# Two units' running sums as products with a triangle, and a written-out order for the first six steps

## The chip, the cores and the metric

The kernel runs on one core of a Trainium2 chip. Its engines are called by the names of the profile: PE (TensorE, the matmuls), DVE (VectorE), ACT (ScalarE), POOL (GpSimd) and SP (SyncE, which here only issues DMAs). Each engine works through its own instructions in the order of the program and waits on semaphores for the others. The metric is the device time of one execution in microseconds (us).

## The reference

A gated linear recurrence is followed by a layer of eight experts, of which each token uses one. B = 4, H = 8 heads, S = 768 tokens, D = 48.

```python
f = 1.0 / (1.0 + np.exp(-f_logit))
for t in range(S):
    state = f[:, :, t, :, None] * state + einsum('bhd,bhe->bhde', k[:, :, t], v[:, :, t])
    y[:, :, t] = einsum('bhd,bhde->bhe', q[:, :, t], state)
x = y.transpose(0, 2, 1, 3).reshape(B * S, H * D)          # (3072, 384)
expert_idx = argmax(x @ w_gate); gate_w = softmax probability of that expert
out = gate_w * (relu(x @ w1[expert_idx]) @ w2[expert_idx])  # F = 1024
```

## The kernel before

The recurrence is computed in blocks of 128 tokens. A **unit** is one block of tokens of two batches with all heads: there are twelve (NU = 12), and unit u continues the state of unit u - 2. In SBUF a unit of q, k and f lies with the channels on the partitions (a pair of heads, each padded from 48 to 64) and eight segments of 128 tokens along the free dimension; v lies with tokens on the partitions. Within a unit the steps are, with the name that the change's list gives each and the function that does it:

- `lf lk lq lv`: the loads (`load`), all on SP's queue. f has two buffers, k three, q four, v three; a load waits until the last reader of its buffer is done.
- `exp`, `ln` (`steps`, `log`; ACT): ln(1 + exp(-f)), which is the negative logarithm of the gate, into a tile g.
- `scan` (`total`; DVE): the running sum of g over the tokens of each segment. One scan of a unit goes over 128 x 1032 elements: each segment has a column of zeros in front, and a minimum with a tile `cap` starts the sum anew there and bounds it.
- `r` and `dec` (`growth`, `decay`; ACT): exp of the sum and exp of its negative.
- `byr` (k times r, POOL, in unit 0 DVE), `byd` (q times decay, DVE). A POOL product waits by hand for a DVE instruction that is known to be a good place (`routed`).
- `ends`, `last` (POOL): the last columns of the sums and of the decay.
- `sc` (`score`; PE): k times q, four PSUM banks; `mask` (DVE): the lower triangle of it is copied by a predicate.
- `kp`, `keep` (`keys` on PE, copied by ACT): k with tokens on the partitions; `dp` (`added`; PE): its product with v, the addition to the state; `upd`, `updp` (`update`; DVE adds, POOL multiplies by the last decay).
- `wi` (`within`; PE, two halves a and b) and `bef` (`before`; PE): the two parts of the output, within the unit and from the state, into one PSUM tile yt; `set` (`settle`; ACT) copies it.
- `xp`, `lay` (`rows` on PE, with a small reduction on DVE for the gate; `lay` on ACT): the output by tokens and the gate's logits.
- `oh`, `wgh`, `place`, `send` (`Route`): the choice of expert for a pair of units, the place of each token's row, and the indirect DMA that sends it there.

Some PSUM tiles (`turns`: kp, dp, xp) take turns on two banks, so each waits for the reader of the last but one.

The units overlap by software: a loop over n = 1 to NU + 1 does, in each turn, the scores of unit n, the sums of unit n + 2, the exp and ln of unit n + 3, the output of unit n - 1 and the rows of unit n - 2, each engine in program order (`manual_schedule`). The steps of units 0 to 3 that lie ahead of the loop are written out before it, and the turns n = 1 and n = 2 differ from the others by conditions. Before the first products PE runs 24 products of a zero tile (`warm`), and 12 more later; their result is not used. The experts' matmuls follow after the loop.

The constants come in three transfers. A mask and the unit matrix are loaded first, through ACT's queue (`load_first_consts`). All others come later, by SP (`load_consts`, L174), and `load_gate` (L180) then writes the gate's weights into the same tile with four small transfers; the first of these waits for the transfer of the constants:

```python
for a, r in halves:
    for b, cols in enumerate((slice(XW, WX), slice(0, E))):
        nc.sync.dma_start(wx[r, :, cols], ...)      # wx is a view of the constants' tile
```

SP's order before: f0, k0, q0, f1, k1, q1, f2, v0, f3, k2, v1, q2, q3, constants, k3, f4, v2, f5, gate, q4, k4, v3, f6, three transfers of `pad` to DRAM, k5, and so on.

Of the kernel before, what the change touches and what calls it, by code (L numbers as in the profile page):

```python
# [10 lines left out]
F32 = mybir.dt.float32  # L11
I32 = mybir.dt.int32
U8 = mybir.dt.uint8
AF = mybir.ActivationFunctionType
OP = mybir.AluOpType
# [12 lines left out]
CR = C + 1  # L28
DM = H * D
# [44 lines left out]
RMAX, RTOP = np.log(1e18), np.log(1e19)  # L74

# [43 lines left out]
def _bc(ap, axis, n):  # L119
    shape = list(ap.shape)  # L120
    shape.insert(axis, n)
    return ap[tuple([slice(None)] * axis + [None])].to_broadcast(shape)
# [3 lines left out]
def kernel(  # L126
# [8 lines left out]
    fu: bass.AP,  # L135
    vu: bass.AP,
# [283 lines left out]

    with ExitStack() as st:
# [9 lines left out]

        cap = wk.tile([128, SEG, CR], F32, name="cap", bufs=1)
        nc.vector.memset(gsum, 0.0)
        nc.vector.memset(cap, RTOP)
        nc.vector.memset(cap[:, :, 0:1], 0.0)
# [8 lines left out]
        for g in decays:  # L444
            nc.vector.memset(g[:, :, 0:1], 0.0)
        units = [{} for _ in range(NU)]
        routed = []
        SYNC = mybir.DependencyInfo(mybir.DependencyClass.Sync, mybir.DependencyReason.DATA)
# [8 lines left out]
        def load(u, names, parts=(slice(None),)):  # L457
            x = units[u]
            for n in names:
                src = {"q": qu, "k": ku, "f": fu, "v": vu}[n]  # L460
                if n == "v":
                    x[n] = ld.tile([128, 2, H, D], F32, name=n, bufs=3)
                else:
                    x[n] = held[n][u % len(held[n])]
                for part in parts:
                    nc.sync.dma_start(x[n][:, part], src[u][:, part])

        whole, ab = slice(0, SEG), (slice(0, HP), slice(HP, SEG))

        def steps(u, part=whole, logs=True):  # L470

            x = units[u]
            x["g"] = decays[u % len(decays)]
            g = x["g"][:, part, 1:CR]
            most = gsum[:, u, 1 if part == ab[1] else 0]
            nc.scalar.activation(
                g, x["f"][:, part], AF.Exp, scale=-1.0, accum_out=most.unsqueeze(1)
            )
            if logs:
                log(u, part)  # L480

        def log(u, part=whole):
            g = units[u]["g"][:, part, 1:CR]
            nc.scalar.activation(g, g, AF.Ln, bias=1.0)  # L484

        def total(u, part=whole):

            x = units[u]
            if "sum" not in x:
                x["sum"] = wk.tile([128, SEG, CR], F32, name="sum")  # L490
            nc.vector.tensor_tensor_scan(  # L491
                x["sum"][:, part].rearrange("p s c -> p (s c)"),
                x["g"][:, part].rearrange("p s c -> p (s c)"),
                cap[:, part].rearrange("p s c -> p (s c)"),
                0.0,
                OP.add,
                OP.min,
            )

        def growth(u, part=whole):  # L500

            x = units[u]
            if "r" not in x:
                x["r"] = wk.tile([128, SEG, C], F32, name="r", bufs=1)
            nc.scalar.activation(x["r"][:, part], x["sum"][:, part, 1:CR], AF.Exp)  # L505

        def by_r(u, part=whole, on=nc.gpsimd):
            k = units[u]["k"][:, part]
            ins = on.tensor_tensor(k, k, units[u]["r"][:, part], op=OP.mult).ins  # L509
            if routed:  # L510

                tc.add_manual_dep(ins, routed.pop().name, SYNC, reason="the port of both")

        def ends(u):
            nc.gpsimd.tensor_copy(rend[:, u], units[u]["sum"][:, :, C])

        def decay(u, part=whole):
            x = units[u]
            x["dec"] = x["g"][:, :, 1:CR]
            nc.scalar.activation(  # L520
                x["dec"][:, part], x["sum"][:, part, 1:CR], AF.Exp, scale=-1.0
            )

        def last_decay(u):
            x = units[u]
            x["last"] = wk.tile([128, SEG], F32, name="last", bufs=3)
            nc.gpsimd.tensor_copy(x["last"], x["dec"][:, :, C - 1])  # L527

        def by_decay(u, part=whole):
            x = units[u]  # L530
            q = x["q"][:, part]
            nc.vector.tensor_tensor(q, q, x["dec"][:, part], op=OP.mult)  # L532
# [32 lines left out]
        def within(u, a):  # L565

            x = units[u]
            if a == 0:
                x["yt"] = yt
            for p, h, _ in heads():  # L570
                nc.tensor.matmul(  # L571
                    x["yt"][DP * (h ^ a) : DP * (h ^ a) + D, a, p],
                    lhsT=x["v"][:, a, 2 * p + h],
                    rhs=x["at"][:, a, h, p],
                    start=p == 0,
                    stop=x["old"] is None,
                    skip_group_check=True,
                )
# [38 lines left out]
        def update(u):  # L617

            x = units[u]
            new = wk.tile([128, SEG, D], F32, name="state", bufs=4)  # L620
            last = _bc(x["last"], 2, D)
            if x["old"] is None:
                nc.vector.tensor_copy(new, x["dp"])
            else:
                nc.vector.tensor_tensor(new, x["dp"], x["old"], op=OP.add)
            states[u % 2] = new
            return lambda: nc.gpsimd.tensor_tensor(new, new, last, op=OP.mult)
# [70 lines left out]
        load(0, "f", ab)  # L698
        load(0, "kq")
        load(1, "f")  # L700
        load_first_consts()
        load(1, "kq")
# [6 lines left out]

        warm(24)  # L710
        for part in ab:
            steps(0, part)
            total(0, part)
        load(2, "f")
        load(0, "v")
        for part in ab:
            growth(0, part)
            by_r(0, part, nc.vector)
            decay(0, part)
            by_decay(0, part)  # L720
        ends(0)
        last_decay(0)
        for part in ab:
            steps(1, part)
        load(3, "f")
        load(2, "k")
        load(1, "v")
        load(2, "q")
        load(3, "q")
# [44 lines left out]
        score(0, 0)  # L774
        score(0, 1)
        keys(0)
        warm(12)
        for part in ab:
            total(1, part)
        for a in range(2):  # L780
            for h in range(2):
                mask(0, a, h)
        for part in ab:
            growth(1, part)
            by_r(1, part)
        for part in ab:
            decay(1, part)
            by_decay(1, part)
        ends(1)
        last_decay(1)  # L790
        steps(2)
        total(2)
        keep(0)
        steps(3, logs=False)
        growth(2)
        load_consts()
        load(3, "k")
        load(4, "f")
        load(2, "v")
        load(5, "f")  # L800
        load_gate()

        for n in range(1, NU + 2):
# [3 lines left out]
            rt = None  # L807
            if here < NU:
                units[here]["old"] = states[here % 2]
            if 2 <= last:  # L810
                settle(last)
            if later and later[0] < NU - 1:
                later[1].weigh()
# [3 lines left out]
            if ahead and n != 2:  # L817
                by_r(n + 1)
                ends(n + 1)
# [7 lines left out]
            if n == 1:  # L827
                units[0]["old"] = None
                added(0)
                update(0)()  # L830
            if ahead and not 1 < n < 4:
                decay(n + 1)
                last_decay(n + 1)
# [3 lines left out]
            if n == 2:  # L837
                growth(n + 1)
                by_r(n + 1)
                ends(n + 1)  # L840
            if 1 < n < 4:
                decay(n + 1)
                last_decay(n + 1)
# [4 lines left out]
            if n == 1:  # L848
                log(3)
                within(0, 0)  # L850
                within(0, 1)
                settle(0)
# [6 lines left out]
            if 2 < n < NU - 2:  # L859
                total(n + 2)  # L860
            if n == NU - 2:
                by_decay(n + 1)
            first_half = 1 < n < NU - 2
            if first_half:
                within(back, 0)
            if 0 <= last:
                rt = rows(last, later[1] if later else None)
                lay(last)
# [6 lines left out]
            if n == 2:  # L875
                total(n + 2)
# [13 lines left out]
            if n == 2:  # L890
                settle(1)
            if n + 2 < NU and n != 1:
                growth(n + 2)
# [7 lines left out]
            if n == 1:  # L901
                total(3)
# [15 lines left out]
            if n == 1:  # L918
                load(n + 3, "q")
# [4 lines left out]
            if 1 < n and n + 3 < NU:  # L924
                load(n + 3, "q")
            if n + 5 < NU:
                load(n + 5, "f")
            if n == 1:
                load_first_pads()
# [398 lines left out]
```

## Time and profile before

| | us |
|---|---|
| median of 10 runs | 390.13 (389.79 to 391.0) |
| the profiled execution | 389.82 |
| its span, first to last instruction | 388.0 |
| PE busy in the span | 375.7 (97%) |
| DVE, ACT, POOL busy | 169.6, 102.9, 115.8 |
| scans (L491), 14 | 28.9 in all; 2.29 a whole one, 1.23 a half |
| DMA until 25 us | about 400 GB/s |

A line of a timeline gives start and duration (us), engine, line of the program, operation, output and inputs, number of instructions, and in brackets how long the engine was idle before and what released it. A line of a chain gives start, duration and what ran. "L491" is line 491 of the kernel before. A matmul in float32 shows as two records.

### The profile page before, as it was taken

To read this page: it belongs to the slowest core of one execution; us is meant where nothing else is said; L and a number is where in the kernel's file an instruction comes from. 1 tells how busy PE (TensorE), PEld (TensorE's weight loads), DVE (VectorE), ACT (ScalarE), POOL (GpSimd) and SP (SyncE) were. 2 spreads that over 40 slices of the span, in tenths; PEclk is the share of its full clock that TensorE was granted. 3 is DMA by queue.
4 is the path that set the end of the run, shared out by engine and by line. 5 is a ranking of instruction groups with operands and counts; after the bars stand their busy time and mean duration, and the time that the engine had idled before them with its cause. 6 is when DMAs were issued, how large, how long until landed. Compare 5 with 4: busy or idle time off the path is not lost.

```text
span 388.0 us, 7727 instructions
## 1 busy us (share of the span) xinstructions
PE 375.7 (97%) x3062; PEld 264.1 (68%) x3062; DVE 169.6 (44%) x365; ACT 102.9 (27%) x190; POOL 115.8 (30%) x118
## 2 busy tenths in 40 slices
PE   7888999999999999999999999999999999999993
PEld 7877899999989778685555555654466466555452
DVE  6998988889764732112121131116412113111360
ACT  6888878785433001010100110000010000001000
POOL 5378868887706610101102101100210210210112
PEclk9999999999999999999999999999999999999998
DMA  7999667778973559795649899898163359994141
GB/s 282 395 364 362 202 228 250 249 240 305 386 247 125 208 135 308 193 318 108 195 148 387 227 394 395 215 399 241 41 231 126 102 181 390 396 416 155 24 182 43
DMA packets 51516, 95.05 MB, mean 245 GB/s; under 512 B 20824, under 2 KB 40731, under 8 KB 49424
## 3 DMA queue, kind: packets, MB, share of 16 engines
q1 hardware_dynamic: 48016, 84.76, 64.1%
q0 software_dynamic: 3168, 9.64, 6.7%
q8 instruction: 25, 0.41, 0.4%
q10 hardware_dynamic: 288, 0.08, 0.2%
q14 instruction: 19, 0.16, 0.1%
HBM read 79.46 MB, written 15.21 MB: 244 GB/s over the span
## 4 chain that ended last, share of the span: by engine, by line
PE 88%; DMA 5%; DVE 2%; ACT 1%; SPq 1%; issue 1%; POOL 0%; POOLq 0%; DVEq 0%; ACTq 0%
PE hps L316 28%; PE yps L332 24%; PE yps L1107 7%; PE xp L663 6%; PE yt L571 5%; PE s L543 4%; PE s L316 3%; PE hps L1081 3%; PE yp L332 3%; PE yt L592 3%; DMA fpack<-c_fpack 2%; PE dp L608 2%; PE kp L558 2%; DMA fpack<-in_moe_w_gate_dram 1%; DVE sum L491 1%; DMA f<-in_fu_dram 1%
## 5 line engine op out<-in xcount | busy, mean ns | idle before, releaser
L316 PE MATMUL hps<-xT,w1t 128*128 128x352 f32 (+2 forms) x384 | 110.1, 447 | 0.0
L316 PEld LDWEIGHTS hps<-xT,w1t 128*128 128x128 f32 x384 | 72.7, 190 | 37.2 <-issue 1.9
L332 PE MATMUL yps<-w2t,hT 128*128 128x384 f32 x288 | 94.4, 487 | 0.0
L189 POOL DMA_INDIRECT out_dram<-ysb,dst x24 | 23.3, 972 | 222.0 <-DVE ysb L343 213.9
L332 PEld LDWEIGHTS yps<-w2t,hT 128*128 128x128 f32 x288 | 54.6, 190 | 38.6 <-issue 1.5
L326 ACT ACTIVATE hT<-hps 128x352 f32<-128x352 f32 (+2 forms) x28 | 13.7, 490 | 200.7 <-PE hps L316 190.6
L328 DVE TENSOR_SCALAR hT<-hps 128x352 f32<-128x352 f32 (+2 forms) x28 | 15.6, 558 | 93.0 <-PE hps L316 93.0
L343 DVE TENSOR_SCALAR ysb<-yps,tg 128x384 f32<-128x384 f32 x22 | 13.6, 618 | 74.4 <-PE yps L332 55.7
L189 POOL DMA_INDIRECT xs<-xr,posi x24 | 32.2, 1342 | 18.9 <-DVE xT L299 12.9
L549 DVE COPY_PREDICATED at<-mpack,s 128x512 f32<-128x512 uint8 x48 | 31.0, 727 | 6.1 <-PE s L543 6.1
L509 POOL TENSOR_TENSOR k<-k,r 128x1024 f32<-128x1024 f32 (+1 forms) x12 | 26.5, 2215 | 19.3 <-ACT r L505 9.9
L491 DVE TENSOR_TENSOR_SCAN sum<-g,cap 128x1032 f32<-128x1032 f32 (+1 forms) x14 | 28.9, 2064 | 2.8 <-ACT g L484 2.8
L1107 PE MATMUL yps<-qw,hqT 128*32 128x192 f32 (+1 forms) x192 | 26.8, 380 | 0.0
L543 PE MATMUL s<-q,k 64*128 64x128 f32 x384 | 24.9, 279 | 1.7 <-POOL last L527 1.1
L663 PE MATMUL xp<-fpack,ys 128*128 128x104 f32 x192 | 25.1, 281 | 0.8 <-DMA fpack<-in_moe_w_gate_dram 0.6
L543 PEld LDWEIGHTS s<-q,k 64*128 64x128 f32 x384 | 22.5, 188 | 3.9 <-issue 1.5
L571 PE MATMUL yt<-at,v 128*48 128x128 f32 x384 | 25.1, 276 | 0.0
L663 PEld LDWEIGHTS xp<-fpack,ys 128*128 128x128 f32 x192 | 22.7, 192 | 2.7 <-issue 1.3
L571 PEld LDWEIGHTS yt<-at,v 128*48 128x48 f32 x384 | 20.0, 123 | 2.6 <-issue 1.5
L1107 PE MATMUL yps<-w2t,hT 128*32 128x384 f32 x192 | 21.4, 487 | 0.0
L1107 PEld LDWEIGHTS yps<-w2t,hT 128*32 128x32 f32 x192 | 7.6, 110 | 13.0 <-issue 12.5
L532 DVE TENSOR_TENSOR q<-q,g 128x1024 f32<-128x1024 f32 (+1 forms) x14 | 16.4, 1178 | 0.0
(114 smaller groups left out, 360.1 us busy)
## 6 DMA issues: line engine op xcount, KB each, us to landing
qw<-in_moe_w_dram SPq DMA_DIRECT2D x16, 1536.0 KB, 13.7
w1t<-in_moe_w_dram SPq DMA_DIRECT2D x8, 1536.0 KB, 7.2
w2t<-in_moe_w_dram SPq DMA_DIRECT2D x8, 1536.0 KB, 15.9
k<-in_ku_dram SPq DMA_DIRECT2D x12, 512.0 KB, 4.9
q<-in_qu_dram SPq DMA_DIRECT2D x12, 512.0 KB, 5.8
f<-in_fu_dram SPq DMA_DIRECT2D x11, 512.0 KB, 6.0
xs<-pad SPq DMA_DIRECT2D x8, 600.0 KB, 4.4
v<-in_vu_dram SPq DMA_DIRECT2D x12, 384.0 KB, 5.9
```

Of the source, the lines that this page charges most:

```text
L189: ins = nc.gpsimd.indirect_dma_start(out=dst, out_offset=bass.IndirectOffsetOnAxis(ap=idx, axis=0), in_=src, in_offset=None, bounds_check= ...
L316: nc.tensor.matmul(x["h"][:, f], lhsT=w[0][:, j, b * 128 : b * 128 + 128], rhs=x["xT"][:, j], start=j == 0, stop=j == KD - 1,)
L328: nc.vector.tensor_scalar(to, x["h"], 0.0, None, op0=OP.max)
L332: nc.tensor.matmul(yp, lhsT=x["hT"][:, f, t * C : t * C + C], rhs=w[1][:, f, :], start=f == 0, stop=f == NF - 1,)
L491: nc.vector.tensor_tensor_scan(x["sum"][:, part].rearrange("p s c -> p (s c)"), x["g"][:, part].rearrange("p s c -> p (s c)"), cap[:, part ...
L509: ins = on.tensor_tensor(k, k, units[u]["r"][:, part], op=OP.mult).ins
L532: nc.vector.tensor_tensor(q, q, x["dec"][:, part], op=OP.mult)
L543: nc.tensor.matmul(ps[h][:, p], lhsT=x["k"][r, s], rhs=x["q"][r, s], start=True, stop=True)
L549: nc.vector.copy_predicated(x["at"][:, a, h], _bc(causal, 1, HP), x["ps", a][h])
L571: nc.tensor.matmul(x["yt"][DP * (h ^ a) : DP * (h ^ a) + D, a, p], lhsT=x["v"][:, a, 2 * p + h], rhs=x["at"][:, a, h, p], start=p == 0, st ...
L663: nc.tensor.matmul(xp[:, p], lhsT=x["ys"][:, a, p], rhs=wx[:, p, 0:XW] if a else wx[:, p, E:WX], start=True, stop=True,)
L1107: nc.tensor.matmul(yp[r], lhsT=h[:, f, at : at + T], rhs=w[:, f, cols], start=f == 0, stop=f == NF - 1, skip_group_check=True,)
```

## The change

f of units 0 and 1 (`NATURAL = 2`) comes from an array `fn` that is laid out with tokens on the partitions, without padding (48 instead of 64 channels), in two halves. exp and ln write it into g with tokens on the partitions, and the running sum is then a product of g with an upper triangle of ones, which also turns it so that the channels lie on the partitions; the sums stay in PSUM, where r and decay read them. The bound of the sum moves into the product with k, as a minimum of r (both halves on DVE, in unit 1 too, where POOL did it before). The tile of ones is cast from the mask by DVE; the g tiles of units 0 and 1 are cleared as a whole.

```diff
-        for g in decays:
+        for g in decays[:NATURAL]:
+            nc.vector.memset(g, 0.0)
+        for g in decays[NATURAL:]:
             nc.vector.memset(g[:, :, 0:1], 0.0)
+        def more_consts():
+            nc.vector.tensor_copy(upto, causal)
+            nc.vector.memset(cap, RTOP)
+            nc.vector.memset(cap[:, :, 0:1], 0.0)
...
+                if n == "f" and u < NATURAL:
+                    flat = x[n].rearrange("p s c -> p (s c)")[:, 0 : SEG * 2 * D]
+                    x["fn"] = flat.rearrange("p (s h d) -> p s h d", s=SEG, h=2)
+                    for part in ab:
+                        nc.sync.dma_start(x["fn"][:, part], fn[u][:, part])
+                    continue
...
+        def summed(u, part):
+            x = units[u]
+            a = ab.index(part)
+            if u:
+                ps = turns("sum", [128, HP, C])
+            else:
+                ps = pss.tile([128, HP, C], F32, name="s")
+            x["sums", a] = ps
+            for p in range(HP):
+                nc.tensor.matmul(
+                    ps[:, p], lhsT=x["g"][:, HP * a + p, 1:CR], rhs=upto, start=True, stop=True
+                )
...
         def by_r(u, part=whole, on=nc.gpsimd):
             k = units[u]["k"][:, part]
+            if u < NATURAL:
+                port["latest"] = nc.vector.scalar_tensor_tensor(
+                    k, units[u]["r"][:, part], RMOST, k, op0=OP.min, op1=OP.mult
+                ).ins
+                return
...
         def ends(u):
-            nc.gpsimd.tensor_copy(rend[:, u], units[u]["sum"][:, :, C])
+            if u < NATURAL:
+                for a, part in enumerate(ab):
+                    nc.vector.tensor_copy(rend[:, u, part], x["sums", a][:, :, C - 1])
+            else:
+                nc.gpsimd.tensor_copy(rend[:, u], x["sum"][:, :, C])
```

The steps ahead of the loop and its turns n = 1 to 5 are gone; in their place stands a list of steps, by the names above with the number of the unit and a half or a part, and the loop begins at n = 6 without its special cases. `fill10` is ten products of the zero tile, `consts0`, `consts1` and `consts2` are the first constants, the other constants and `more_consts`, `gate` is `load_gate`, `pads` the transfers of `pad`. Each engine and queue takes its own steps in the order of the list:

```diff
+    FIRST_STEPS = """
+        consts0 lf0 lk0 lq0 lf1 lk1 lq1 consts2 fill10 exp0a ln0a scan0a exp0b lf2 lv0 ln0b scan0b
+        r0a byr0a dec0a byd0a r0b byr0b dec0b byd0b ends0 last0 exp1a ln1a exp1b lf3 lk2 lv1
+        lq2 lq3 consts1 gate0 ln1b sc0a scan1a scan1b sc0b r1a dec1a r1b dec1b mask0a byr1a
+        ends1 byd1a byr1b byd1b last1 sc1a fill2 kp0 mask0b exp2 ln2 keep0 scan2 exp3 r2
+        sc1b byr2 ends2 dp0 lk3 lf4 lv2 lf5 upd0 upd0p dec2 last2 kp1 lq4 lk4 keep1 mask1a
+        mask1b ln3 wi0a wi0b lv3 set0 exp4 lf6 pads0 byd2 dp1 upd1 scan3 sc2a upd1p kp2 sc2b
+        keep2 r3 ends3 byr3 dec3 last3 mask2a mask2b exp5 wi1a xp0 lay0 ln4 ln5 byd3 scan4
+        wi1b lk5 lv4 lq5 lf7 set1 r4 dp2 upd2 sc3a sc3b scan5 byr4 ends4 kp3 keep3 dec4
+        last4 mask3a mask3b exp6 ln6 wi2a wi2b lk6 lv5 xp1 lay1 byd4 oh1 r5 bef2 lq6 lf8 dp3
+        upd3 set2 wgh1 sc4a sc4b byr5 upd2p ends5 dec5 last5 kp4 keep4 mask4a mask4b scan6
+        exp7 ln7 wi3a xp2 lay2 byd5 place1 wi3b lk7 lv6 r6 dp4 upd4 bef3 lq7 lf9 set3 sc5a
+        sc5b byr6 upd3p ends6 upd4p dec6 last6 kp5 keep5 mask5a mask5b scan7 exp8 ln8 wi4a
+        wi4b lk8 lv7 xp3 lay3 byd6 oh3 r7 bef4 lq8 lf10 dp5 upd5 set4 wgh3 send5
+    """
...
+        for what, u, part in re.findall(r"([a-z]+)(\d+)([abp]?)", FIRST_STEPS):
+            DO[what](int(u), part)
...
-        for n in range(1, NU + 2):
+        for n in range(FIRST, NU + 2):
```

## The prediction

> **What bounds the kernel now.** I read the page first, then the chain of waits up to 60 us, then the timelines of PE, DVE, ACT and SP over the same stretch, and the DMA landings. On the page PE is busy for 97% of the span, and the chain that ended last is 88% PE. The room is in the first two of the forty slices. The chain says where it ends:
>
> ```profile
> 40.99 0.17 DVE lg L671
> 41.16 0.02 issue
> 41.19 0.49 ACT xr L693
> 41.67 0.04 issue
> 41.72 1.14 PE dp L608 x32
> 42.86 1.02 PE yt L592 x32
> 43.88 1.99 PE s L543 x32
> 45.86 1.02 PE kp L558 x8
> ```
>
> Up to 41.7 us the chain runs over DMA, ACT and DVE; from there every line to 108 us is PE, without a gap, one unit of the recurrence after the other. So a change in the first six steps is worth exactly what it does to the time at which PE takes up its closed row. I use one mark for this: the scores of unit 4 (43.81 us on PE's timeline). From there the order of PE's work is the same in both kernels but for a swap of neighbours, 18.37 us to the scores of unit 6, and then the same loop.
>
> What holds the row up before the mark is a group of full engines (in the slices 10:40 us DVE is busy 4.2 to 5.0 us of each 5, ACT 4.25 to 4.6) and the DMA queue, which moves about 400 GB/s until 25 us. The SP timeline, start, duration, queue and line, has the part that decides my forecast:
>
> ```profile
> 13.88 1.06 SPq L174 DMA_DIRECT2D fpack<-c_fpack  x1
> 15.06 0.37 SPq L466 DMA_DIRECT2D k<-in_ku_dram  x1
> 15.90 0.33 SPq L466 DMA_DIRECT2D f<-in_fu_dram  x1
> 16.75 0.33 SPq L466 DMA_DIRECT2D v<-in_vu_dram  x1
> 19.00 0.33 SPq L466 DMA_DIRECT2D f<-in_fu_dram  x1
> 22.76 1.79 SPq L180 DMA_DIRECT2D fpack<-in_moe_w_gate_dram  x4
> 24.65 0.39 SPq L466 DMA_DIRECT2D q<-in_qu_dram  x1
> ```
>
> SP's waits and the landings of two of these transfers (KB, us from issue to landing):
>
> ```profile
> SPq L180 <- DMA fpack<-c_fpack: 3.4, 1, 3.4
> fpack<-c_fpack SPq DMA_DIRECT2D x1, 473.5 KB, 8.9
> f<-in_fu_dram SPq DMA_DIRECT2D x1, 512.0 KB, 9.4
> ```
>
> The gate weights go into the tile that the constants fill, so SP stands still until the constants have landed (13.88 + 8.9 = 22.74), and what is behind in SP's program stands with it: q of unit 4 leaves at 24.65 although its buffer was free long before. But k3, f4, v2 and f5 are ahead of the gate and leave from 15.06 on. f4 lands at 15.90 + 9.4 = 25.3, and that already is a wait on ACT:
>
> ```profile
> 23.28 1.07 ACT L633 COPY ys<-yt 128x512 f32<-128x512 f32 x2
> 25.39 1.06 ACT L476 ACTIVATE g<-f 128x1024 f32<-128x1024 f32 x1 [1.04 <-DMA f<-in_fu_dram]
> 26.57 1.06 ACT L484 ACTIVATE g<-g 128x1024 f32<-128x1024 f32 x1
> ```
>
> **The change, part by part.**
>
> *Sums as products.* DVE loses four half scans of 1.23 us, 4.9 us. It gains k times r of unit 1 (two halves, 0.67 each by L509 on DVE, from POOL, where the two took 2.84), four copies of a last column and a cast of the triangle (0.1 to 0.2 each by the small copies, 0.7 in all). Net about 2.8 us off DVE. ACT: exp and ln of 384 instead of 512 elements take 0.48 instead of 0.63 (the 128x384 copy of L693), eight of them, 1.2 us. PE: 16 products, 32 records; 16 records of L663 take 1.96, so 1.0 per half and 4.0 in all, against 24 warm-up products fewer (48 records; the last 24 took 2.85). The memsets of two whole g tiles (0.92 each) lie before 4 us, ahead of the first exp at 3.6, and cost nothing; without that cover 1.8.
>
> *Where this would leave the first steps.* The ten warm-up products are not done at once: records 1 to 13 or so come at 0.2 us, the later ones at 0.113, so they end near 5.8 and the first sum at 6.9, where the first exp of sums now starts at 6.66. Unit 0 gains nothing. In unit 1 ACT's four exp and ln end at 11.15 instead of 11.75, and the 0.64 us wait for the scan goes: exp of unit 2 starts near 13.5 instead of 14.74, scan2 at 16.0 instead of 17.07, and mask, copies and ys of unit 0 each about 1.1 us earlier. ACT is through ys of unit 0 at 23.2 instead of 24.35. What is late next is f4.
>
> *The loads, re-ordered.* The written order puts the constants and the gate directly behind q3, and k3, f4, v2, f5, q4, k4 and v3 behind the gate. On SP they are all moved past a wait that they were ahead of. The constants land a little earlier: f of two units is 256 KB smaller (0.26 MB at some 405 GB/s, 0.65 us), so 22.1. It could be earlier by more, as nothing is queued behind them: at 22.74 the queue had moved 7.85 MB, 0.8 MB (2 us) more than was issued up to the constants, while the loads until 14 us landed with 0.37 MB (0.9 us) of such excess. That bounds the landing by 20.1 and 22.1; I take 21.6, nearest to the early loads. The gate's four issues hold SP for 1.89 (22.76 to 24.65), then k3 leaves at 23.5 and f4 at 23.95, into a queue that has run dry. Later in the trace f was issued right behind q in such a queue twice (43.94 and 44.36, 53.31 and 53.73) and landed 4.8 and 4.6 us after issue. The gate's own small packets go ahead of k3; in 25:28 us, with them, the queue moved 262 to 303 GB/s instead of some 405, which is 0.9 us lost, of which 0 to 0.5 would fall on k3. So f4 lands at L = 28.7, with bounds 27.0 and 29.7, against 25.3 now. It is queued ahead of everything on ACT: behind exp of unit 4 stand the copy of unit 2's keys, both exp of unit 3, exp of unit 5, rows of unit 0.
>
> *From f4 to the mark.* ACT in its new order, start to start by the rows of before: exp4 1.18, kn2 0.95, r3 0.95, decay3 0.95, exp5 1.18 (f5 lands 2.3 behind f4, in time), rows of unit 0 0.78, ln4 0.96: 6.95, and 0.05 to DVE: L + 7.0. DVE: scan4 2.22 and the state of unit 2 0.53: L + 9.75. PE has to wait for that state, as the second half of unit 3's keys takes the PSUM tile that it frees; then half the keys 0.5, two halves of unit 2's yt 2.0, xp of unit 1 1.96, the state's part of yt 1.02, dp of unit 3 1.05: 6.55, and the mark at L + 16.3. DVE beside it: scan5 2.29, four masks 2.5, gate sums 0.3 and q of unit 4 1.2 end at L + 16.0. Both branches end together, so neither can shorten it alone. At L = 28.7 the mark is at 45.0 instead of 43.81: +1.2 us. All that units 0 and 1 gained or lost before 23.2 goes into a wait of 5.5 us on ACT and is worth nothing; if f4 were there, ACT could start 2.2 us earlier than now. Contention adds 0 to 0.6 (one scan of before took 2.93 beside a POOL product, instead of 2.29).
>
> *A gap on PE.* PE has its first half of yt of unit 1 done near 26.9 and xp of unit 0 needs a PSUM tile that ACT's copy frees at L + 1.65 = 30.35: 3.4 us idle, where the longest idle of before was 1.1. What such a gap does to PE's rate no row of before shows; from the start of the trace (0.2 us per record in the first 3 us, then 0.113) the bounds are 0 and some 1.4 us over the 16 records. PE then has until L + 9.75 for xp, half of yt, dp, scores and half the keys, 6.5 us of work in 8.1; so I take 0, and up to 0.6 at the upper end. The Trainium skill, "TensorE: Matmul & The Clock Gate", Part 1 on the clock gate, says that an idle window of about 3.4 us halves PE's clock until as much sustained work has passed; by that rule the gap is on the edge, and since the slack holds the 1.4 us, the sum by the rule is still +1.2.
>
> **The sum.** The profiled execution took 389.82 us, its span is 388.0, with 1.8 around it; the median is 390.13. The rest of the span after the mark, 344.2, stays. 389.82 + 1.2 = 391.0 for a profiled execution, and 390.13 + 1.2 = 391.3 for the median.
>
> **The rivals.**
>
> A, faster: f4 is not late. For this the constants would have to land by some 20 us, or the loads to be held less by the gate. The mechanism is the one from which the rest follows: what counts is only L, and it decides at L = 27.5, where the mark is back at 43.8. If f4 came 0.65 before its present 25.3, the sum above gives 24.65 + 16.3 = 40.95, 2.9 us gained: 387.3. Against it: SP's wait of 3.4 us and q4's issue behind it stand in the trace; even the lowest bound, 27.0, gives 43.3 and only 0.5 gained. 15 in 100.
>
> B, no difference: f4 is late, but near its lower end (L of 27.2 to 27.9), as the constants land without company: 390.1. 12 in 100.
>
> C, slower still: PE's rate falls after the gap and the two scans run beside POOL's work, both of which are bounded above: L = 29.3 gives 45.6, plus 0.6 and 0.6, 46.8: +3.0, 393.1. 11 in 100.
>
> **How the numbers follow.** The forecast, L between 27.9 and 29.7 with the sum as it stands, gives +0.4 to +2.2 and has 62 in 100. A measurement of this kernel tells 0.2%, 0.8 us, from no change. Of the forecast 9 fall within that and 53 above; of A 13 below and 2 within; B is within, C above. Faster 0.13, same 0.23, slower 0.64. The range, 389.4 to 393.0, takes in the forecast, B, the weaker part of A and most of C, and leaves out some 17 in 100. The likeliest case's own range is 390.5 to 392.3.
>
> **What the changed profile would show.** On SP the four issues of the gate near 21.6, and k3 and f4 directly behind them at 23.5 to 24.0. On ACT one long wait for f, about 5 us, that ends near 28.7, and before it every step of units 0 to 2 earlier by 1 us. DMA running dry in 21:25 us. On PE a gap of some 3.4 us before the first L663-like product, and the scores of unit 4 at 45.0, without gaps after it. DVE with ten scans instead of fourteen. I am wrong if ACT's wait for f4 ends before 27.5, if the steps between it and unit 4's scores take other than 16.3 us, or if gaps come back after the mark.

## The result, and the profile after

The changed kernel takes 393.27 us (392.49 to 394.52, 9 runs) against 390.10 (30 runs): ratio 1.0084, 95% interval 1.0073 to 1.0095, 3.2 us slower. Its profiled execution took 392.67 with a span of 390.6, against 389.82 and 388.0.

In the lines below f4 is the f of unit 4 (the load `lf4`). `ys` is what `set` copies, `kn` what `keep` copies (kn2 is unit 2's), and `xr` are the rows that `lay` copies. The first steps' lines have other numbers in each kernel.

SP's timeline after the change (start, duration, queue, line, transfer):

```profile
13.57 0.43 SPq L178 DMA_DIRECT2D fpack<-c_fpack  x1
22.63 2.75 SPq L184 DMA_DIRECT2D fpack<-in_moe_w_gate_dram  x4
25.49 0.38 SPq L499 DMA_DIRECT2D k<-in_ku_dram  x1
25.96 0.38 SPq L499 DMA_DIRECT2D f<-in_fu_dram  x1
26.39 0.42 SPq L499 DMA_DIRECT2D v<-in_vu_dram  x1
26.86 0.42 SPq L499 DMA_DIRECT2D f<-in_fu_dram  x1
```

SP's longest wait (us in all, times, longest):

```profile
SPq L184 <- DMA fpack<-c_fpack: 8.5, 1, 8.5
```

And f4's way from issue to landing (KB, us):

```profile
f<-in_fu_dram SPq DMA_DIRECT2D x1, 512.0 KB, 4.2
```

SP issues nothing from 14.0 to 22.6 us. f4 leaves at 25.96 instead of 15.90 and lands at 30.1 instead of 25.3. The stretches 20:23 show the DMA running dry meanwhile. Each row gives the stretch, its length, the busy us of the five engines with counts, the clock granted to PE, and in the last two columns the share of the 16 DMA engines and GB/s:

```profile
20.00:21.00 1.00, 0.93 (x8) 0.67 (x7) 1.00 (x2) 1.00 (x2) 0.21 (x1) 1.00 0.73 284
21.00:22.00 1.00, 1.00 (x18) 0.86 (x18) 1.00 (x3) 1.00 (x2) 1.00 (x1) 1.00 0.22 87
22.00:23.00 1.00, 1.00 (x26) 1.00 (x22) 1.00 (x3) 1.00 (x3) 1.00 (x1) 1.00 0.02 8
```

ACT's timeline: the wait for f4 grew from 1.0 to 5.7 us, and the copies of unit 2's keys follow it.

```profile
23.46 1.07 ACT L700 COPY ys<-yt 128x512 f32<-128x512 f32 x2
30.20 1.06 ACT L515 ACTIVATE g<-f 128x1024 f32<-128x1024 f32 x1 [5.67 <-DMA f<-in_fu_dram]
...
31.25 1.05 ACT L630 COPY kn<-kp 128x512 f32<-128x512 f32 x2
```

PE's timeline, from the gap to the scores of unit 4:

```profile
27.61 1.08 PE L637 MATMUL yt<-at,v 128*48 128x128 f32 x16
31.87 3.13 PE L730 MATMUL xp<-fpack,ys 128*128 128x104 f32 x16 [3.19 <-ACT kn L630]
34.93 1.58 PE L637 MATMUL yt<-at,v 128*48 128x128 f32 x16
...
46.43 2.06 PE L610 MATMUL s<-q,k 64*128 64x128 f32 x32
```

In the kernel before, the same rows of unit 0 and the same scores stand at

```profile
28.93 2.00 PE L663 MATMUL xp<-fpack,ys 128*128 128x104 f32 x16 [0.62 <-DMA fpack<-in_moe_w_gate_dram]
...
43.81 2.06 PE L543 MATMUL s<-q,k 64*128 64x128 f32 x32
```

The mark, the scores of unit 4, is at 46.43 instead of 43.81: 2.62 us later. The span is 2.6 longer, so all of it arises before the mark; after it PE has no wait over 0.2 us in either kernel.

### The profile page after: what moved, and what is told of

Same layout as the page of the kernel before. It is cut to its first block, busy times and chain, and to the rows that moved or that the text cites. A ratio compares the mean times of both kernels' runs of the same rounds, so it can differ in the third digit from the quotient of the medians.

```text
span 390.6 us, 7692 instructions
## 1 busy us (share of the span) xinstructions
PE 375.9 (96%) x3046; PEld 264.1 (68%) x3046; DVE 168.1 (43%) x368; ACT 101.3 (26%) x190; POOL 108.2 (28%) x114
## 4 chain that ended last, share of the span: by engine, by line
PE 90%; DMA 4%; issue 1%; POOL 1%; ACT 1%; SPq 1%; POOLq 0%; DVE 0%; ACTq 0%
PE hps L320 28%; PE yps L336 24%; PE yps L1168 7%; PE xp L730 6%; PE yt L637 5%; PE s L610 5%; PE s L320 3%; PE hps L1142 3%; PE yp L336 3%; PE yt L658 3%; PE dp L674 2%; PE kp L625 2%; DMA f<-in_fn_dram 2%; DMA k<-in_ku_dram 2%; DMA f<-in_fu_dram 1%
## 5 line engine op out<-in xcount | busy, mean ns | idle before, releaser
L573 POOL TENSOR_TENSOR k<-k,r 128x1024 f32<-128x1024 f32 x10 | 23.8, 2375 | 24.6 <-ACT r L564 6.4
L730 PE MATMUL xp<-fpack,ys 128*128 128x104 f32 x192 | 26.3, 289 | 3.4 <-ACT kn L630 3.2
L730 PEld LDWEIGHTS xp<-fpack,ys 128*128 128x128 f32 x192 | 23.7, 199 | 5.3 <-ACT kn L630 3.4
L1168 PE MATMUL yps<-qw,hqT 128*32 128x192 f32 (+1 forms) x192 | 26.8, 380 | 0.0
L550 DVE TENSOR_TENSOR_SCAN sum<-g,cap 128x1032 f32<-128x1032 f32 x10 | 24.2, 2418 | 0.3 <-POOL xr L722 0.3
L599 DVE TENSOR_TENSOR q<-q,g 128x1024 f32<-128x1024 f32 (+1 forms) x14 | 15.5, 1104 | 0.6 <-DMA q<-in_qu_dram 0.6
```

The source lines that it names most:

```text
L550: port["latest"] = nc.vector.tensor_tensor_scan(x["sum"][:, part].rearrange("p s c -> p (s c)"), x["g"][:, part].rearrange("p s c -> p (s ...
L599: port["latest"] = nc.vector.tensor_tensor(q, q, x["dec"][:, part], op=OP.mult).ins
L730: nc.tensor.matmul(xp[:, p], lhsT=x["ys"][:, a, p], rhs=wx[:, p, 0:XW] if a else wx[:, p, E:WX], start=True, stop=True,)
L1168: nc.tensor.matmul(yp[r], lhsT=h[:, f, at : at + T], rhs=w[:, f, cols], start=f == 0, stop=f == NF - 1, skip_group_check=True,)
```

## The experiments

All came from the theory that the loads held behind the gate make the loss. For each kernel I read the time against the kernel before on its own chip, and the mark in its profile. One kernel profiled twice had its mark at 41.94 and 42.29, so 0.35 us of a mark mean nothing.

**The gate behind f5 again** (`e1`):

```diff
-        lq2 lq3 consts1 gate0 ln1b ...
+        lq2 lq3 consts1 ln1b ...
-        sc1b byr2 ends2 dp0 lk3 lf4 lv2 lf5 upd0 ...
+        sc1b byr2 ends2 dp0 lk3 lf4 lv2 lf5 gate0 upd0 ...
```

> The changed kernel with one step of its list moved: the gate's four loads stand behind f5 again, so that k3, f4, v2 and f5 leave before SP stops for the constants. No instruction of PE, DVE, ACT or POOL changes its place. Theory (the loads behind the gate make the whole loss): f4 lands near 25.2 instead of 30.1, ACT's wait of 5.7 us shrinks to under 1, the scores of unit 4 come 16.3 us after it, at 41.5 instead of 46.4, and the time is 388 us, 2 below the kernel before. Rival (the new order of the steps or the products with the triangle cost the time themselves, PE gets 16 products more): the time stays above 391 though f4 comes early.

Measured 388.38 us against 389.86, ratio 0.9963 (0.9950 to 0.9976): faster than both kernels. Its ACT timeline at exp of unit 4, and its PE timeline:

```profile
25.13 1.06 ACT L515 ACTIVATE g<-f 128x1024 f32<-128x1024 f32 x1 [0.30 <-DMA f<-in_fu_dram]
```

```profile
28.92 2.03 PE L730 MATMUL xp<-fpack,ys 128*128 128x104 f32 x16
...
42.13 2.06 PE L610 MATMUL s<-q,k 64*128 64x128 f32 x32
```

The order of SP's queue alone is worth 4.3 us at the mark, and 1.2% by the two ratios. The gap on PE and the halved rate behind it are gone with it (2.03 us for the same 16 records).

**The gate early in the kernel before** (`e2`): the same move alone, with the old order and the scans.

```diff
         load_consts()
+        load_gate()
         load(3, "k")
...
-        load_gate()
```

> The kernel before with only this changed: the gate's loads are issued directly behind the constants, ahead of k3, f4, v2 and f5. Theory: SP stops near 22.7, f4 lands near 30 instead of 25.3, ACT waits about 5.7 us for it, and the scores of unit 4 come 3 to 4.7 us later, 393 to 395 us in all. Rival (the new order costs it, not the loads): within 1 us of the kernel before.

Measured 395.37 us, ratio 1.0147 (1.0132 to 1.0161); ACT waits for f4 until 30.3 and the mark is at 49.15, 5.3 us late, more than I expected.

```profile
30.32 1.06 ACT L476 ACTIVATE g<-f 128x1024 f32<-128x1024 f32 x1 [5.17 <-DMA f<-in_fu_dram]
```

So this one move costs the written order 4.3 us at the mark and the old one 5.3. f4 is taken up about 5 us later in both (30.2 instead of 25.1, 30.3 instead of 25.4). From there to the mark the written order then takes 16.2 instead of 17.0 us, and the old one 18.8 instead of 18.4: the written order gets a part of the delay back, the old one does not.

**The written order with scans** (`e3`): `e1` with the products with a triangle taken out (`NATURAL = 0`; the array `fn` stays unused).

> The changed kernel with the gate's loads behind f5, and without the products with a triangle: units 0 and 1 load f by channels and sum by scans on DVE, all in the written order. Theory (what comes before f4 is worth nothing while f4 decides): f4 lands near 25.2 as with the products, ACT is through its work before it at 24.4 to 25.2, and the time is within 0.5 us of the run with the products, near 388. Rival (the products bring what gain there is): 1 us or more slower than the run with the products.

Measured 392.11 us, ratio 1.0050 (1.0033 to 1.0066), mark 45.53: slower than the kernel before (43.81) too. My expectation was wrong: the products are worth 3.4 us at the mark here. f4 was not as early as I had put it either: the issue of k3 waited 6.1 us for PE's keys of unit 0, so f4 left at 21.33 and landed at 26.8; ACT took it up at 27.71, without a wait. PE's timeline shows where the delay begins:

```profile
10.00 3.79 PE L611 MATMUL s<-q,k 64*128 64x128 f32 x32 [3.29 <-DVE q L600]
15.93 2.08 PE L611 MATMUL s<-q,k 64*128 64x128 f32 x16 [2.15 <-POOL rend L585]
...
18.96 1.91 PE L626 MATMUL kp<-fpack,k 128*128 128x128 f32 x8
```

PE works at about half rate (keys of unit 0 in 1.91 us; 1.04 in `e9`) after gaps of 3.3 and 2.2 us, where the run with products had sums. I read this from the times of the records: the granted clock on the profile is 1.00 in these stretches. In `e7`, where the same keys take the same 1.91, it is 0.50.

**k times r on DVE** (`e7`): `e3` with k times r of unit 1 on DVE.

```diff
-            by_r(u, piece(part), nc.gpsimd if u else nc.vector)
+            by_r(u, piece(part), nc.gpsimd if u > 1 else nc.vector)
...
-            routed[:] = [port["latest"]] if u else []
+            routed[:] = [port["latest"]] if u > 1 else []
```

> The run with the written order, the gate behind f5 and the scans (392.1), with k times r of unit 1 on DVE instead of POOL. Theory (of that run's 3.7 us over the run with the products, the larger part is POOL's slow k times r, which the scores of unit 1 and behind them the keys of unit 0 wait for): the scores of unit 1 start a little later than there, but PE keeps its rate, the keys of unit 0 are copied 1.5 us earlier, 390 to 391.2 in all. Rival (the scans on DVE make the 3.7 us): 392 or more.

The mark is at 45.78, no better than 45.53. The move did not make the product earlier: on DVE its first half stands behind the masks and ends at 15.47, where POOL's ended at 15.17, and PE kept to the low rate. So this shows that the move brings nothing, not that POOL's product is no part of the delay. In `e5` to `e11` PE stands idle for 4.1 to 6.2 us between 120 and 140 us, and its granted clock is 0.69 to 0.84 over that stretch; in the runs up to `e4` and in the two kernels' profiles it is not idle there. The kernel before took 401 to 402 us beside them. What PE waits for there is not shown, so their times say less than their marks. Measured 403.73 us, ratio 1.0061 (1.0035 to 1.0088).

**Scans, with PE kept busy** (`e9`): `e3` with products of the zero tile where the triangle's had been.

```diff
-        ... lq1 consts2 fill10 exp0a ...
+        ... lq1 consts2 fill24 exp0a ...
-        ... ln1b sc0a scan1a scan1b sc0b r1a ...
+        ... ln1b sc0a fill8 scan1a scan1b sc0b fill12 r1a ...
```

> The run with the written order, the gate behind f5 and the scans (its scores of unit 4 came at 45.5), with more products of the zero tile: 24 at the start instead of 10, 8 behind the first and 12 behind the second half of unit 0's scores, where the triangle's products kept PE busy. Theory (without the triangle's products PE's rate falls, so that the scores of unit 1 and the keys of unit 0 take twice as long, and this makes most of the 3.4 us between the two): the keys of unit 0 take 1.1 instead of 1.9 us and are done 2 us earlier, the scores of unit 4 come at 43 to 43.7. Rival (the scans on DVE and k times r on POOL are the delay): the scores of unit 4 at 45 or later.

```profile
16.89 1.16 PE L611 MATMUL s<-q,k 64*128 64x128 f32 x16
...
18.53 1.04 PE L626 MATMUL kp<-fpack,k 128*128 128x128 f32 x8
...
43.53 2.06 PE L611 MATMUL s<-q,k 64*128 64x128 f32 x32
```

The mark is at 43.53 as the theory said; 401.70 us, ratio 0.9999 (0.9975 to 1.0024). With PE kept busy the written order with scans is about where the old order is (43.81). Of the 3.4 us that the products are worth in the written order, useless products bring 2.0, by keeping PE at its rate. That is the least that the rate is worth: the useless products also hold up the scores of unit 1, which start right behind them at 16.89 instead of 15.93. At most 1.4 is left for the sums themselves.

**Fewer warm-up products in the kernel before** (`e11`): 10 and 2 instead of 24 and 12.

> The kernel before with 10 and 2 products of the zero tile instead of 24 and 12, the numbers of the written order. Theory: PE is idle from 6 to 9.3 us, its rate falls, the scores and keys of unit 0 take 3.8 and 1.9 instead of 2.4 and 1.1, and the scores of unit 4 come 0.5 to 2 us after 43.8. Rival (at this place PE has slack, and DVE and ACT set the pace): within 0.4 us of the kernel before.

Here the rival held: the first scores take 3.78 us and the keys 1.97, but the mark is at 43.96, 0.15 late. Measured 403.29 us, ratio 1.0033 (0.9999 to 1.0068), not clear of no change; the 0.15 is less than a mark can tell. In the old order the keys of unit 0 stand ahead of the scores of unit 1, and the path does not show the low rate; the written order put them behind, and PE's rate became part of its path.

**A warm gap** (`e5`): the changed kernel with twelve useless products in PE's gap ahead of xp of unit 0.

> The changed kernel, and in PE's gap ahead of xp of unit 0 twelve products of the zero tile into a free bank of the scores, so that PE is idle for some 2 us instead of 4. Theory (the late f4 alone sets the loss, PE has slack after the gap): xp of unit 0 takes 2.0 instead of 3.1 us, the scores of unit 4 still come 16.3 us after f4, and the time stays within 0.5 us of the changed kernel's 393.3. Rival (PE's halved rate after the gap costs a part): 1 us or more faster than 393.3.

```profile
31.73 2.03 PE L730 MATMUL xp<-fpack,ys 128*128 128x104 f32 x16 [0.22 <-ACT kn L630]
...
35.52 1.14 PE L674 MATMUL dp<-v,kn 128*64 128x48 f32 x32 [0.75 <-ACT xr L760]
```

xp takes 2.03 instead of 3.13, and the time saved turns into a wait of dp for ACT's copy. f4 is taken up at 30.05, the mark is at 46.29, 16.2 behind it; 405.19 us, ratio 1.0094 (1.0064 to 1.0125), no gain over the changed kernel's 1.0084. The halved rate after this gap costs nothing that a mark can tell.

**f4 alone ahead of the gate** (`e8`): in the changed kernel only f4 is issued before SP stops.

> The changed kernel with f4 alone moved ahead of the gate; k3, v2 and f5 stay behind it. Theory (each load costs what it is late for its reader): f4 lands by 24 and ACT does not wait for it; k3 leaves near 25.5 and lands near 28.8, f5 lands near 31.5, 3 us after ACT is ready for it, and the scores of unit 4 come 12.3 us after that, at 43.8, so about the time of the kernel before, 389.4 to 390.8. Rival (f4 was the whole loss): 388.4, like the run with the gate behind f5.

```profile
24.94 1.09 ACT L515 ACTIVATE g<-f 128x1024 f32<-128x1024 f32 x1
...
33.17 1.06 ACT L515 ACTIVATE g<-f 128x1024 f32<-128x1024 f32 x1 [3.27 <-DMA f<-in_fu_dram]
```

The wait for f4 is gone and f5's has taken its place; f5 was taken up 1.6 us later than I had put it, and the mark is at 46.30, as in the changed kernel. From f5 to the mark it took 13.1 us where I had 12.3: after another gap PE is slow again.

```profile
34.74 1.75 PE L674 MATMUL dp<-v,kn 128*64 128x48 f32 x32 [2.54 <-ACT xr L760]
36.41 3.00 PE L610 MATMUL s<-q,k 64*128 64x128 f32 x32
```

The same steps take 1.14 and 2.06 at the full rate. Ratio 1.0077 (1.0047 to 1.0107), 404.74 us. Here the next load behind the gate is late for its own reader, and moving the first alone brings nothing.

**Loads in another order** (`e4`, `e6`, `e10`): in `e4` f4 stands directly behind the constants, q3 and k3 behind f4; in `e6` the constants stand behind f3, and then k2, v1, q2, f4, k3, v2, gate, f5, q3. `e10` is `e6` once more.

> As the first run, and f4 directly behind the constants, q3 and k3 behind f4. Theory: f4 lands by 24, before ACT is ready for it at 24.5, so the step after ys of unit 0 no longer waits; the scores of unit 4 come at 24.5 + 16.3 = 40.8, 0.6 us before those of the first run, near 387.4 in all. Rival (by then another wait has taken over, xp of unit 0 for the gate or a load that was put back): the same as the first run within 0.2 us or slower.

```profile
30.07 2.00 PE L730 MATMUL xp<-fpack,ys 128*128 128x104 f32 x16 [1.20 <-DMA fpack<-in_moe_w_gate_dram]
```

`e4`: 388.74 us, ratio 0.9961 (0.9948 to 0.9974), mark 43.25. That is 1.1 us behind the mark of `e1` at the same ratio; the profiled execution was the slowest of its six, so this mark is not typical of the median. f4 is no longer waited for; xp waits for the gate's weights, which land last at 29.9. The rival held.

> The changed kernel with other places for seven loads: the constants directly behind f3, then k2, v1, q2, then f4, k3, v2, the gate, f5, and q3 last. Theory: the constants land near 18, so SP never stops for them; f4 lands by 24.3 and the gate by 26; neither is waited for, PE runs from the scores of unit 2 on without a gap but for the state of unit 2, and the time is 387.9 to 388.4, that of the run with the gate behind f5 or 0.4 less. Rival (something that was hidden, such as k2 or q2, which now come 1.3 us later, is waited for): 389 or more.

> The kernel with the constants directly behind f3 and the gate ahead of f5 once more, since in its first run PE's granted clock fell for all kernels at 130 us and hid the difference: by the scores of unit 4 at 41.94 it should take 0.9952 of the kernel before (1.9 of 390), and not less gain than the run with the gate behind f5 (0.9963).

`e6`: 401.18 us, ratio 0.9992 (0.9971 to 1.0013), mark 41.94; `e10`: 400.86, 0.9981 (0.9954 to 1.0009), mark 42.29. Both missed what I expected: I had `e6` at a ratio of about 0.995, and the interval of `e10` leaves out the 0.9952 that I had for it. Neither f4 nor the gate is waited for, yet the mark is that of `e1`, 42.13: in `e6` ACT now waits 0.66 us for unit 2's keys. As far as these waits show, what bounds the first steps is then the row of scores, keys and copies on PE and ACT; no run took that row apart. The faster versions by a clear interval are `e1` and `e4`.

## Why the prediction was right or wrong

**Direction and mechanism: right.** The loss is the gate's wait on SP, as forecast: `e1` takes it away and the kernel is faster, `e2` makes it alone and the old kernel is slower. The size was wrong, +1.2 against +3.2, and the range ended 0.3 below the result. The step that failed is L, f4's landing: it makes 1.4 of the missing 2.0 us. The other 0.55 had no term in the sum at all (see the last part of this section).

**L, the mis-sized term.** I put f4's landing at 28.7 with an upper bound of 29.7; it was 30.1. By its parts: the constants landed at 22.6, not 21.6 (+1.0); from there to k3's issue it took 2.9, not 1.9 (+1.0); f4's own way took 4.15, not 4.7 (-0.55).
- *The constants.* I argued that with nothing queued behind them they would land up to 2 us sooner. In `e1`, where k3, f4 and v2 are queued behind them, they landed no later, at 13.92 + 8.6 = 22.5:

```profile
fpack<-c_fpack SPq DMA_DIRECT2D x1, 473.5 KB, 8.6
```

Wherever they stand behind q2 and q3 they landed between 21.7 (`e7`) and 23.2 (`e8`), with loads queued behind them or without. Nor does my 21.6 follow from my own figures: with the 0.9 us of excess of the early loads in place of the 2 us, they give 21.0. In the rows 20:23 above, what remains of the transfers ends over 2 us at a falling rate: the last part to finish sets the landing. That the 0.8 MB which I took for company were later transfers on DMA engines that were already through is the reading that fits both runs; single engines were not looked at. The 0.65 us for the smaller f did not come either: from 4 to 8 us the queue moved 254 to 363 GB/s, where it was 336 to 414 before, and f3's issue, which waits for exp of unit 1, moved from 11.23 to 11.29. In `e1`, with the same loads in the same order, it moved 379 from 4 to 8 us, so why it was slower here is open.
- *The gate's issues.* Of the four, one took 1.39 us instead of 0.44. The four took 1.8 to 1.9 us in the kernel before, `e1`, `e4`, `e9` and `e11`, and 2.5 to 3.1 in the other runs. In all four runs whose queue had run dry (the changed kernel, `e2`, `e5`, `e8`) one of the four took 1.2 to 1.4 us, but some runs with a full queue took as long. The prediction took 1.89 from a full queue. I found no cause.

**From f4 to the mark: right.** 46.43 - 30.11 = 16.3, the predicted sum, and 16.2 in `e5`. The scan of unit 4 starts at L + 7.0, as forecast, and the state of unit 2 is done at 39.86, L + 9.75:

```profile
37.10 2.31 DVE L550 TENSOR_TENSOR_SCAN sum<-g,cap 128x1032 f32<-128x1032 f32 x1 [0.31 <-POOL xr L722]
```

So the sum was right by its parts, and not by luck.

**A wait that I left out.** In the kernel before f4 was not the only late arrival: the gate's weights landed at 28.84, and xp of unit 0 waited 0.62 us for them. It cost the sum nothing, as f4 was later still, but `e4` met it (1.20 us).

**The first steps: wrong, and it cost nothing.** ACT should have been through ys of unit 0 at 23.2; it was at 24.5, against 24.35 before. exp of unit 2 began at 14.04 instead of 13.5, and the copy of unit 0's keys then waited 1.06 for PE, since the written order has the keys behind the scores of unit 1. With f4 at 30.1 this was hidden, as I had said of all that units 0 and 1 gained or lost. In `e1` it is not: f4 and ACT come together at 25.1, and kn2 and rows of unit 0 wait for PE, so the way to the mark is 17.0 and not 16.3.

**The products.** I had counted them as 4.0 us of PE against fewer warm-up products and 2.8 us less on DVE. That they keep PE's rate up was not in my sum; `e3` and `e9` make it the larger part of their worth where f4 is not held back by the gate.

**The gap on PE: right.** 3.2 us of idle, then 0.196 us per record instead of 0.125; the granted clock over the first 43.8 us is 0.96, 1.00 before. The slack swallowed it (`e5`). The Trainium skill, "TensorE: Matmul & The Clock Gate", Part 1, gives an idle window of about 3.4 us after which the clock is halved. The gaps here were shorter: 3.19 us in this kernel (granted clock 0.50 from 34 to 36 us) and 2.54 in `e8` (0.50 from 36 to 38 us). After 2.16 in `e4` the full rate stayed. The measurements decide: the rate can fall after an idle time shorter than the page's window. The gap of 2.2 us in `e3` followed a slow stretch, so that gap alone is not shown to bring it.

**The rivals.** A's condition was made in `e1`: 388.4 where I had put 387.3. C's time came out, 393.1, but not its mechanism: neither the scans nor PE's rate added anything to the 16.3.

**Between mark and median.** Of the 3.17 us, 2.62 are at the mark, 0.25 lie outside the span (2.07 instead of 1.82), and 0.3 lie between the profiled execution and the median of the runs. In the profiles of all kernels with the list, the one with `NATURAL = 0` too, 1.93 to 2.14 us lie outside the span, and 1.72 to 1.90 in the kernel before and its variants `e2` and `e11`: so the 0.25 go with the list, whatever its loads and with or without the products; which part of it makes them was not tested. The 0.3 stay open.

## What to carry to other kernels

A wait in a queue that issues transfers is charged to every transfer behind it, each by how late it is for its own reader; so when transfers are put into a new order, look first for the one that waits on another transfer, and put what needs no wait ahead of it, as far as its own reader allows: in `e4` the gate's weights then came late. A transfer that must land before something can be issued should be timed by its slowest part, as it landed before, and not by when the queue's bytes were through. A path through one late arrival can be summed closely from a profile even when what lies ahead of it is judged wrongly, so most of the care belongs to that arrival.

## What the runs showed that I had not expected

Useless products on PE were worth 2.0 us in the written order (mark 45.53 and 43.53) and 0.15 in the old one (43.96 and 43.81), less than a mark can tell: what a falling PE rate costs depends on whether PE's first products are on the path. And a DMA queue that was left to run dry needed 1.6 us, 21.0 to 22.6, for its last 0.1 MB (87 and 8 GB/s in the rows 21:23), so here draining it cost more than the missing bytes say.
